# A later planned place for two kinds of stores, and a last product, join and store in two halves of rows

## The chip, the cores and the metric

One core of a Trainium2 chip runs the whole program. The metric is the time of one execution on the device, in microseconds (us); the runs of a kernel are given by their median. A profile of one more execution gives the trace. TensorE (PE) does the matmuls, VectorE (DVE) and ScalarE (ACT) the elementwise work, GpSimd (POOL) a little, and SyncE (SP) issues every DMA of this kernel from one queue, in order.

## The reference, cut to what matters

```python
x = chunk_attention(q, k, v)            # 8 x 8 heads, 576 tokens, chunks of 64, head size 64
x = concat_heads(x)                     # 8 x 576 x 512: 4608 tokens of 512
xn = layernorm(x) * g_ln
x = x + relu(xn @ w_ch1) @ w_ch2        # 512 -> 2048 -> 512
gate = sigmoid(causal_conv5(x, conv_w)) # five taps per channel, along the tokens
out = (gate * (x @ w_val)) @ w_out      # 512 -> 512 -> 512
```

All of it is float32. Every product is made from operands split into a high and a low part, with three matmuls (high by high, high by low, low by high).

## The kernel before, in words

**Blocks.** The 4608 tokens are nine blocks of 512. Blocks 0 and 1 go through the feed-forward layer with plain products. Blocks 2 to 8 use a scheme of seven products of half-size matrices in place of eight: `hidden` for the first matrix, and in the last stage `val` for `w_val` and `proj` for `w_out`. One such product is `twelve` (L1248): two column halves `f` of the left operand, two `k`, three high and low pairs, so 12 matmuls of 256 columns into one PSUM tile of 512 columns, 256 for each `f`. With the tokens' operand on the left, as in `proj`, `f` is the half of the rows (128 tokens each) of the result.

**What is stored and read again.** When a block leaves the feed-forward layer, `conv(b)` (L1613) works on its rows X in the background of the next blocks. For each of four groups of channels ScalarE starts the sum of taps in a room `u0` or `u1` (L1638), VectorE adds the other taps (L1645), and a store puts the result, the gate before its sigmoid, into DRAM (L1658). The next group but one takes the same room and must wait until that store has landed. `seven` (L1434) makes the block's seven operands for `val`: VectorE subtracts quadrants into `t` (L1454), ScalarE takes the high part (L1472), VectorE the low part (L1477), and a store puts the operand into DRAM (L1482); three rooms (`SPLITS`) take turns. Block 0 does the same later from a stored copy (`seven_again`, `conv_again`, stores at L1482 and L1600). When conv and operands of block b are done, X is free for block b + 2, whose attention tiles are copied there (L813 on ScalarE, L826 on GpSimd). `hidden` loads the half-size parts of the feed-forward weights again for each block (L1327, `late_a<-a`).

**What sets the order.** Nothing is ordered by hand. A planner (`Plan.run`, L55) simulates the engines: each operation has an engine, a duration, a priority (`pri`, a due time) and operations that it depends on. At each planned moment a free engine takes the ready operation of lowest priority value, and its instructions are emitted then; so the planned times set the order of every engine's queue, SP's among them, and the chip runs each queue in that order. Between an operation and one that waits for it on another engine the planner puts a fixed time:

```python
HOP = {"PE": 220.0, "DVE": 80.0, "ACT": 80.0, "POOL": 200.0, "SP": 3500.0}
wait = 0.0 if a.eng == (e,) else max(self.HOP[e], self.HOP["PE"] if "PE" in a.eng else 0.0) + op.more
if e == "SP":
    wait += a.slack
```

So a store is planned 80 ns behind VectorE's last operation on it. A store of the conv is planned at 728 ns and taken as landed 3500 ns behind that; one of an operand at 1300 ns and landed 3500 + 2000 ns behind that (its `more`).

**The end.** `proj(8)` does its seven products in the order 1, 5, 6, 3, 7, 4, 2. The last three results are: `c21` of product 4, copied by ScalarE and stored with `c22` as the lower 256 tokens (512 KB); `c12`, stored alone (256 KB); and `c11`: product 2 in the bank of `yB`, one VectorE operation that adds it to what ScalarE had copied (`join`, L1990), and one store of 256 tokens by 256 columns (256 KB, L1999).

Of the kernel before, what the change touches and what calls it, by code (L numbers as in the profile page):

```python
# [15 lines left out]
ALU = mybir.AluOpType  # L16
AX = mybir.AxisListType

P = 128
# [1 line left out]


class Op:
    __slots__ = ("eng", "dur", "fn", "deps", "pri", "left", "after", "ready", "seq", "xfer", "more", "slack")

    def __init__(self, eng, dur, fn, deps, pri, seq):
        self.eng, self.dur, self.fn, self.pri, self.seq = eng, dur, fn, pri, seq
        self.deps = [d for d in dict.fromkeys(deps) if d is not None]
        self.after, self.ready, self.xfer, self.more, self.slack = [], 0.0, None, 0.0, 0.0


class Plan:
# [10 lines left out]
    def add(self, eng, dur, fn, deps=(), pri=0.0, xfer=None):  # L43
        op = Op(eng if isinstance(eng, tuple) else (eng,), dur, fn, deps, pri, len(self.ops))
        op.xfer = xfer
        self.ops.append(op)
        return op
# [5 lines left out]
    def hold(self, tag, *ops):  # L53
        self.held[tag] = list(ops)

    def run(self):
        for op in self.ops:
            op.left = len(op.deps)
            for d in op.deps:
                d.after.append(op)  # L60
        free = {e: 740.0 if e == "SP" else 0.0 for op in self.ops for e in op.eng}
        ready = {e: [] for e in free}
        events = []
        done = set()

        def offer(op):
            for e in op.eng:
                heapq.heappush(ready[e], (op.pri, op.seq, op))

        for op in self.ops:  # L70
            if not op.left:
                offer(op)
        t, n, moved, landed = 0.0, 0, 0.0, []
        while n < len(self.ops):
            for e in free:
                if free[e] > t:
# [12 lines left out]
                dur = op.dur[op.eng.index(e)] if isinstance(op.dur, tuple) else op.dur  # L89
                end = t  # L90
                for x, parts in op.xfer or ():
                    flying = landed[-self.LANES :]
                    if len(flying) == self.LANES:
                        end = max(end, flying[0][0])
                    for l, _ in flying:
                        if sum(m for z, m in flying if z > end) + parts > self.RING:
                            end = max(end, l)
                    turn = self.TURN if parts == P and landed and landed[-1][1] != P else 0.0
                    end += dur
                    moved = max(end + self.LAG, moved + turn) + x  # L100
                    landed.append((moved, parts))
                if not op.xfer:
                    end = t + dur
                free[e] = end
                if len(op.eng) > 1:
                    op.fn(e)
                else:
                    op.fn()
                n += 1
                for a in op.after:  # L110
                    if op.xfer:
                        wait = moved - end
                    else:
                        wait = 0.0 if a.eng == (e,) else max(self.HOP[e], self.HOP["PE"] if "PE" in a.eng else 0.0) + op.more
                        if e == "SP":
                            wait += a.slack
                    a.ready = max(a.ready, end + wait)
                    a.left -= 1
                    if not a.left:
                        heapq.heappush(events, (a.ready, a.seq, a))  # L120
                heapq.heappush(events, (free[e], -1, None))
            if n == len(self.ops):
                break
            t = max(t, events[0][0])
            while events and events[0][0] <= t:
                op = heapq.heappop(events)[2]
                if op is not None:
                    offer(op)
# [3 lines left out]
def chunk_attention_ffn_gated_conv(  # L132
# [21 lines left out]
    nc = tc.nc  # L154
# [1090 lines left out]
        for kk in range(KD):  # L1245
            hold(f"W{g}_{kk}", *(last_use[g, x] for x in range(KD)), *reads)

    def twelve(ps, left, right, new):  # L1248


        for f in range(2):
            for k in range(2):
                lh, ll = (left(s, k)[:, f * P : (f + 1) * P] for s in range(2))
                for i, (l, r) in enumerate(((lh, 0), (lh, 1), (ll, 0))):
                    nc.tensor.matmul(  # L1255
                        ps[:, f],
                        l,
                        right(r, k),
                        start=new and f == k == i == 0,
                        stop=k == 1 and i == 2,  # L1260
                        skip_group_check=True,
                    )
# [169 lines left out]
    def seven(b, quad, reads, pri):  # L1432
# [29 lines left out]
        def split(i, m, src, *deps):  # L1462
            rt, sp = SPLITS[n_split[0] % 3], {}
            n_split[0] += 1

            def sources():
                return quad(*src) if src else [(0, HB, st["t"])]

            def high():
                sp["t"] = slot(rt, [P, 2, 2, HB], F32R, f"x7_{b}_{m}")  # L1470
                for lo, hi, a in sources():
                    nc.scalar.activation(out=sp["t"][:, 0, :, lo:hi], in_=a, func=AF.Copy)  # L1472

            def low():
                t = sp["t"]
                for lo, hi, a in sources():
                    nc.vector.tensor_tensor(  # L1477
                        out=t[:, 1, :, lo:hi], in0=a, in1=t[:, 0, :, lo:hi].bitcast(F32), op=ALU.subtract
                    )

            def store():
                nc.sync.dma_start(out=x7_dram[b, m].bitcast(F32), in_=sp["t"].bitcast(F32))  # L1482

            oh = add("ACT", 680, high, list(deps) + take(rt), pri)
            ol = add("DVE", 690, low, [oh], pri)
            x7_store[b, m] = add("SP", 1300, store, [ol], pri)
            x7_store[b, m].more = 2000.0
            hold(rt, x7_store[b, m])
            if src:
                last.setdefault(src, []).append(ol)  # L1490
            return ol
# [79 lines left out]
    def conv_again(f):  # L1571
# [35 lines left out]
            oa = add("DVE", 760, more(i), [oa], pri)  # L1607
        hold(rt, oa)
        conv_store[0, f] = add("SP", 728, keep, [oa], pri)
        hold(at, conv_store[0, f])  # L1610

    def conv(b):
# [19 lines left out]
        for f in range(KD if b else 0):  # L1632
# [31 lines left out]
                oa = add("DVE", 760, more(i), [oa], pri)  # L1664
            last.append(oa)
            conv_store[b, f] = add("SP", 728, keep, [oa], pri)
            hold(at, conv_store[b, f])
        if b == 0:
            x2_store[b] = add("SP", 2900, store, done, pri)
# [289 lines left out]
    def proj(jj):  # L1959
# [1 line left out]
        pri = B0 + SET * (jj + 1) + 5 * M_TIME  # L1961
        st, ends = {}, jj == NBLK - 1

        def product(m, into, new, deps):
            def go():
                if new:
                    st[into] = half_of(f"y{into.upper()}", f"o{j}_{m}")
                twelve(st[into], gv_o[j, m], wo[m], new)

            at = pri + 2 * M_TIME * (LAST_ORDER if ends else P_ORDER).index(m)  # L1970
            o = add("PE", 1385, go, [gv_op[j, m]] + wo_op[m] + deps, at)
            hold(gv_room[j, m], o)
            return o

        rooms = [OUT_RING[(out_n[0] + x) % len(OUT_RING)] for x in (0, 2 if ends else 1)]
# [11 lines left out]

            return add("ACT", 620, go, list(deps), pri - 1e7)

        def join(into, h, f, *deps):  # L1990
            def go():
                nc.vector.tensor_tensor(out=o(h, f), in0=o(h, f), in1=st[into], op=ALU.add)

            return add("DVE", 700, go, deps, pri - 1e7)

        def store(h, x, *deps):
            def go():
                r0 = j * NB + h * NB // 2
                nc.sync.dma_start(  # L1999
                    out=out[r0 : r0 + NB // 2, x].rearrange("(i p) d -> p i d", p=P), in_=st["o", h][:, :, x]  # L2000
                )

            hold(rooms[h], add("SP", 1300, go, deps, pri))
# [12 lines left out]
        store(1, slice(0, DM), c21, c22)  # L2016
        m3 = product("3", "b", False, [m5, s5])
        c12 = join("b", 0, 1, m3, u2)
        m2 = product("2", "b", True, [c12])
        c11 = join("b", 0, 0, m2, s1)  # L2020
        hold("yA", c21)
        hold("yB", c11)
        if ends:
            store(0, slice(DM // 2, DM), c12)
            store(0, slice(0, DM // 2), c11)
        else:
            store(0, slice(0, DM), c11, c12)


    g_op = ln_scale()  # L2030
# [80 lines left out]
```

## Time and profile before

| what | us |
|---|---|
| runs: median (lowest to highest of 3) | 1070.41 (1068.2 to 1075.63) |
| the profiled execution's own time | 1070.03 |
| its span in the trace | 1068.2 |
| PE busy in the span | 1053.9 |

The span runs from the first to the last instruction of the trace; 1.83 us of the profiled execution lie around it. A busy time is the time in which an engine had an instruction in work; matmuls overlap one another in it. In a row of waits the figures are the sum in us, the number of times and the longest one.

### The profile page before, as it was taken

Reading aid. Unit: us, or ns where it says so; the run is one execution under the profiler, and the core shown is the slowest. Engines: PE = TensorE matmul, PEld = TensorE weight load, DVE = VectorE, ACT = ScalarE, POOL = GpSimd, SP = SyncE. Lnnn points to the kernel's source line nnn. Section 1 sums busy time; section 2 is a strip of 40 time slices with the busy share of each in tenths; the row PEclk is TensorE's granted clock in tenths of the full one; section 3 lists DMA queues with packets and bytes.
Section 4 is the critical chain, followed back from the end, with each engine's and each line's share of the span. In section 5 each row is a group of like instructions: output and inputs, shape, how many; then the busy total and the mean of one; then the engine's idle time right before and its main releaser. Section 6 shows DMA issues by size and latency. Waiting matters only on the chain.

```text
span 1068.2 us, 22725 instructions
## 1 busy us (share of the span) xinstructions
PE 1053.9 (99%) x8950; PEld 951.4 (89%) x8950; DVE 856.4 (80%) x1464; ACT 540.3 (51%) x871; POOL 40.4 (4%) x77
## 2 busy tenths in 40 slices
PE   9999999999999999999999999999999999999998
PEld 8988888888899988889888898899898989999998
DVE  5888978888885888767878877878756889998785
ACT  5796634435354445445445543544443555655553
POOL 1011000000000000000000000000000000000000
PEclk9999999999999999999999999999999999999999
DMA  8995358667999899989989989998976988999852
GB/s 193 289 368 175 108 159 252 220 179 207 246 329 270 233 297 337 282 242 344 278 260 329 299 233 233 352 282 250 319 234 203 381 330 305 309 334 377 316 206 80
DMA packets 205905, 284.14 MB, mean 266 GB/s; under 512 B 99278, under 2 KB 151014, under 8 KB 205798
## 3 DMA queue, kind: packets, MB, share of 16 engines
q1 hardware_dynamic: 205798, 282.68, 84.6%
q8 instruction: 71, 1.16, 0.5%
q14 instruction: 36, 0.29, 0.1%
HBM read 207.64 MB, written 67.63 MB: 258 GB/s over the span
## 4 chain that ended last, share of the span: by engine, by line
PE 88%; DMA 4%; issue 2%; DVE 2%; ACT 2%; SPq 1%; POOL 0%; DVEq 0%; ACTq 0%; POOLq 0%
PE m L1255 24%; PE o L1255 8%; PE v L1255 8%; PE y L1034 7%; PE yA L1412 5%; PE yA L1414 5%; PE yB L1412 5%; PE yB L1414 4%; PE yA L1413 4%; PE yB L1413 4%; PE att L631 3%; PE att L604 3%; PE h L1010 3%; PE h L1012 2%; PE h L1011 2%
## 5 line engine op out<-in xcount | busy, mean ns | idle before, releaser
L1255 PEld LDWEIGHTS m<-late,late_a 128*128 128x128 f32 x2352 | 296.3, 188 | 22.5 <-DVE c_hl L1354 6.1
L1255 PE MATMUL m<-late,late_a 128*128 128x256 f32 x2352 | 303.3, 280 | 7.1 <-DMA late_a<-a 3.1
L1645 DVE SCALAR_TENSOR_TENSOR u_room<-X,cw_sb,u_room 128x516 f32<-128x516 f32 (+1 forms) x128 | 95.1, 747 | 10.4 <-ACT u_room L1638 7.9
L1034 PE MATMUL y<-hh,w 128*128 128x512 f32 x224 | 70.9, 398 | 0.0
L1354 DVE TENSOR_TENSOR c_hh<-c_hh,m 128x512 f32<-128x512 f32 x56 | 38.4, 685 | 36.6 <-PE m L1255 22.9
L1347 ACT ACTIVATE c_hh<-m 128x512 f32<-128x512 f32 x56 | 33.4, 596 | 54.9 <-PE m L1255 54.7
L1412 PE MATMUL yA<-late_h,w 128*128 128x512 f32 x148 | 59.4, 401 | 0.0
L1412 PE MATMUL yB<-late_h,w 128*128 128x512 f32 x148 | 59.0, 399 | 0.0
L1414 PE MATMUL yB<-late_h,w 128*128 128x512 f32 x148 | 58.1, 393 | 0.0
L1414 PE MATMUL yA<-late_h,w 128*128 128x512 f32 x148 | 58.0, 392 | 0.0
L1413 PE MATMUL yA<-late_h,w 128*128 128x512 f32 x148 | 58.0, 392 | 0.0
L1413 PE MATMUL yB<-late_h,w 128*128 128x512 f32 x148 | 57.8, 390 | 0.0
L1034 PEld LDWEIGHTS y<-hh,w 128*128 128x128 f32 x224 | 40.8, 188 | 8.4
L1287 ACT ACTIVATE late<-xs 128x512 fp32r<-128x512 f32 x49 | 30.4, 628 | 35.1 <-PE m L1255 20.6
L1010 PE MATMUL h<-xnt,w 128*128 128x512 f32 x112 | 45.4, 405 | 0.0
L770 POOL TENSOR_TENSOR rstd<-ve,neg_half 128x1 f32<-128x1 f32 x36 | 24.7, 687 | 541.8 <-DVE ve L750 541.4
L1012 PE MATMUL h<-xnt,w 128*128 128x512 f32 x112 | 44.2, 395 | 0.0
L1011 PE MATMUL h<-xnt,w 128*128 128x512 f32 x112 | 44.2, 394 | 0.0
L1034 PE MATMUL y<-hl,w 128*128 128x512 f32 x112 | 44.0, 393 | 0.0
L1382 ACT ACTIVATE late_h<-c_hh 128x512 fp32r<-128x512 f32 x38 | 23.9, 630 | 38.9 <-DVE c_hh L1354 38.2
L678 ACT ACTIVATE p<-p 128x512 f32<-128x512 f32 x33 | 20.8, 630 | 41.6 <-DVE p L670 23.6
L699 ACT ACTIVATE pT<-px 128x1024 uint16<-128x1024 uint16 x28 | 38.5, 1374 | 6.3 <-DMA px<-ps 6.1
(272 smaller groups left out, 2440.0 us busy)
## 6 DMA issues: line engine op xcount, KB each, us to landing
late_a<-a SPq DMA_DIRECT2D x196, 512.0 KB, 5.6
x7d<-late_x SPq DMA_DIRECT2D x42, 512.0 KB, 5.9
late_a<-x7d SPq DMA_DIRECT2D x39, 512.0 KB, 5.4
raw<-in_moe_w_ch_dram SPq DMA_DIRECT2D x32, 512.0 KB, 7.6
late<-x7d SPq DMA_DIRECT2D x24, 512.0 KB, 5.5
qk_room<-in_q_dram SPq DMA_DIRECT2D x100, 112.0 KB, 5.2
qk_room<-in_k_dram SPq DMA_DIRECT2D x100, 112.0 KB, 4.1
x7d<-x SPq DMA_DIRECT2D x21, 512.0 KB, 5.6
```

Of the source, the lines that this page charges most:

```text
L699: nc.scalar.activation(out=t.bitcast(U16).rearrange("p (x s) -> p s x", s=2), in_=st["turned"], func=AF.Copy)
L1010: nc.tensor.matmul(ps, wh, xh, start=(kk == 0), stop=False)
L1011: nc.tensor.matmul(ps, wh, xl, start=False, stop=False)
L1012: nc.tensor.matmul(ps, wl, xh, start=False, stop=(kk == KD - 1))
L1034: nc.tensor.matmul(ps, w[:, s], x, start=opens and n == 0, stop=closes and n == 2, skip_group_check=not b)
L1255: nc.tensor.matmul(ps[:, f], l, right(r, k), start=new and f == k == i == 0, stop=k == 1 and i == 2, skip_group_check=True,)
L1347: nc.scalar.activation(out=st[tag], in_=st[into], func=AF.Copy)
L1354: nc.vector.tensor_tensor(out=st[tag], in0=st[tag], in1=y, op=op)
L1412: nc.tensor.matmul(ps, wh, hh, start=opens and f == 0, stop=False)
L1413: nc.tensor.matmul(ps, wl, hh, start=False, stop=False)
L1414: nc.tensor.matmul(ps, wh, hl, start=False, stop=closes and f == 3)
L1645: nc.vector.scalar_tensor_tensor(out=a, in0=X[b][:, f, i : i + L], scalar=cw_sb[:, i, f : f + 1], in1=a, op0=ALU.mult, op1=ALU.add,)
```

## The change

Operations get a field `behind`, zero by default. Where an operation of another engine than SP ends, each operation that waits for it is planned later by its own `behind`. Three kinds of store get 2000 ns: the operands of `seven` (63 stores), the gates of `conv` and those of `conv_again` (36 stores, some in two DMAs). In the last block `proj` makes product 2 as two operations of six matmuls, one for each half of the rows; behind each half stand a VectorE join of 128 partitions by 256 elements and a store of 128 KB. The other blocks keep the product whole.

```diff
                         if e == "SP":
                             wait += a.slack
+                        else:
+                            wait += a.behind
...
             x7_store[b, m] = add("SP", 1300, store, [ol], pri)
+            x7_store[b, m].behind = 2000.0
             x7_store[b, m].more = 2000.0
...
         conv_store[0, f] = add("SP", 728, keep, [oa], pri)
+        conv_store[0, f].behind = 2000.0
...
             conv_store[b, f] = add("SP", 728, keep, [oa], pri)
+            conv_store[b, f].behind = 2000.0
...
-    def twelve(ps, left, right, new):
-        for f in range(2):
+    def twelve(ps, left, right, new, sides=(0, 1)):
+        for f in sides:
...
-            o = add("PE", 1385, go, [gv_op[j, m]] + wo_op[m] + deps, at)
-            hold(gv_room[j, m], o)
+            o = add("PE", 1385 * len(sides) // 2, go, [gv_op[j, m]] + wo_op[m] + deps, at)
+            if 1 in sides:
+                hold(gv_room[j, m], o)
...
-                nc.vector.tensor_tensor(out=o(h, f), in0=o(h, f), in1=st[into], op=ALU.add)
+                t = o(h, f)[:, side]
+                nc.vector.tensor_tensor(out=t, in0=t, in1=st[into][:, side], op=ALU.add)
...
         if ends:
             store(0, slice(DM // 2, DM), c12)
-            store(0, slice(0, DM // 2), c11)
+            m2 = product("2", "b", True, [c12], (0,))
+            c11 = join("b", 0, 0, m2, s1, side=slice(0, 1))
+            store(0, slice(0, DM // 2), c11, side=slice(0, 1))
+            m2 = product("2", "b", True, [m2], (1,))
+            c11 = join("b", 0, 0, m2, s1, side=slice(1, 2))
+            store(0, slice(0, DM // 2), c11, side=slice(1, 2))
         else:
+            m2 = product("2", "b", True, [c12])
+            c11 = join("b", 0, 0, m2, s1)
             store(0, slice(0, DM), c11, c12)
```

## Rows read from the trace of the kernel before

**Rows 1.** The page: its first line and the busy times by engine.
```profile
span 1068.2 us, 22725 instructions
...
PE 1053.9 (99%) x8950; PEld 951.4 (89%) x8950; DVE 856.4 (80%) x1464; ACT 540.3 (51%) x871; POOL 40.4 (4%) x77
```

**Rows 2.** Waits of PE, whole span: us in total, times, longest.
```profile
PE m L1255 <- DMA late_a<-a: 3.1, 2, 1.6
PE m L1255 <- DVE c_hl L1354: 2.1, 3, 1.0
...
PE m L1255 <- DVE c_hh L1354: 0.5, 1, 0.5
```

**Rows 3.** Waits of SP's queue, whole span.
```profile
SPq L1482 <- DVE late_x L1477: 12.3, 15, 1.8
...
SPq L1658 <- DVE u_room L1645: 9.7, 7, 2.4
...
SPq L1525 <- DMA gd<-u_room: 3.3, 1, 3.3
```

**Rows 4.** Line 1658, the conv's stores: issues and landing.
```profile
L1658 SPq DMA_DIRECT2D gd<-u_room x60: 319/422/1597, 268.7 to 948.3; - x60
...
DMA to landing us min/median/max: 2.5/4.7/7.6
```

**Rows 5.** Timeline, 670 to 679 us: start, us, engine, line, operation [idle before].
```profile
670.99 0.86 SPq L1658 DMA_DIRECT2D gd<-u_room  x2
...
671.95 0.44 SPq L1327 DMA_DIRECT2D late_a<-a  x1
...
678.15 3.06 PE L1255 MATMUL m<-late,late_a 128*128 128x256 f32 x24 [1.46 <-DMA late_a<-a]
```

**Rows 6.** Timeline of SP, 389 to 391 us.
```profile
389.31 0.38 SPq L1525 DMA_DIRECT2D u_room<-x2d  x1
389.78 0.89 SPq L1658 DMA_DIRECT2D gd<-u_room  x2
390.77 0.42 SPq L1327 DMA_DIRECT2D late_a<-a  x1
```

**Rows 7.** Waits, all engines, whole span: ScalarE for the conv's room.
```profile
ACT u_room L1638 <- DMA gd<-u_room: 25.8, 10, 5.8
```

**Rows 8.** Timeline, 549 to 562 us.
```profile
552.98 0.87 SPq L1658 DMA_DIRECT2D gd<-u_room  x2
...
558.48 0.73 ACT L1638 ACTIVATE u_room<-X,cw_sb 128x516 f32<-128x516 f32 x1 [2.39 <-DMA gd<-u_room]
...
561.45 0.74 PE L1255 MATMUL m<-late,late_a 128*128 128x256 f32 x4 [0.49 <-DVE c_hh L1354]
```

**Rows 9.** Timeline, 467 us: PE.
```profile
467.42 1.69 PE L1255 MATMUL m<-late,late_a 128*128 128x256 f32 x12 [0.96 <-DVE c_hl L1354]
```

**Rows 10.** Timeline of the end, 1062 to 1068.2 us.
```profile
1062.67 1.57 PE L1255 MATMUL o<-w,late_gv 128*128 128x256 f32 x12
...
1063.49 0.37 SPq L1999 DMA_DIRECT2D out_dram<-os  x1
1064.28 0.69 DVE L1992 TENSOR_TENSOR late_os<-late_os,o 128x512 f32<-128x512 f32 x1 [2.14 <-PE o L1255]
1065.00 0.37 SPq L1999 DMA_DIRECT2D out_dram<-late_os  x1
```

**Rows 11.** DMA issues, 1060 to 1068.2 us: number, KB each, us to landing.
```profile
out_dram<-late_os SPq DMA_DIRECT2D x2, 256.0 KB, 2.2
out_dram<-os SPq DMA_DIRECT2D x1, 512.0 KB, 2.8
```

**Rows 12.** Groups by line and shape: a VectorE operation of 256 elements out of PSUM.
```profile
L844 DVE TENSOR_TENSOR xnt<-att,xnt 128x256 fp32r<-128x256 f32 x8 | 3.0, 418 | 0.5 <-ACT X L813 0.3
```

**Rows 13.** Timeline, 675 to 690 us: last use of X, next block's last tile.
```profile
675.55 0.55 DVE L1454 TENSOR_TENSOR t<-X 128x384 f32<-128x384 f32 x1
...
689.99 0.60 PE L604 MATMUL att<-ident,x 128*128 128x128 f32 x4
```

More of the change, by code (lines that the diff above doesn't have):

```diff
@@ L23 @@
 class Op:
-    __slots__ = ("eng", "dur", "fn", "deps", "pri", "left", "after", "ready", "seq", "xfer", "more", "slack")
+    __slots__ = ("eng", "dur", "fn", "deps", "pri", "left", "after", "ready", "seq", "xfer", "more", "slack", "behind")
     def __init__(self, eng, dur, fn, deps, pri, seq):
@@ L28, in __init__ @@
         self.deps = [d for d in dict.fromkeys(deps) if d is not None]
-        self.after, self.ready, self.xfer, self.more, self.slack = [], 0.0, None, 0.0, 0.0
+        self.after, self.ready, self.xfer, self.more, self.slack, self.behind = [], 0.0, None, 0.0, 0.0, 0.0
 class Plan:
@@ L1962, in proj, with product @@
         st, ends = {}, jj == NBLK - 1
-        def product(m, into, new, deps):
+        def product(m, into, new, deps, sides=(0, 1)):
             def go():
-                if new:
+                if new and 0 in sides:
                     st[into] = half_of(f"y{into.upper()}", f"o{j}_{m}")
-                twelve(st[into], gv_o[j, m], wo[m], new)
+                twelve(st[into], gv_o[j, m], wo[m], new, sides)
             at = pri + 2 * M_TIME * (LAST_ORDER if ends else P_ORDER).index(m)
-            o = add("PE", 1385, go, [gv_op[j, m]] + wo_op[m] + deps, at)
-            hold(gv_room[j, m], o)
+            o = add("PE", 1385 * len(sides) // 2, go, [gv_op[j, m]] + wo_op[m] + deps, at)
+            if 1 in sides:
+                hold(gv_room[j, m], o)
             return o
@@ L1988, in shot, with join, store @@
             return add("ACT", 620, go, list(deps), pri - 1e7)
-        def join(into, h, f, *deps):
+        def join(into, h, f, *deps, side=slice(0, 2)):
             def go():
-                nc.vector.tensor_tensor(out=o(h, f), in0=o(h, f), in1=st[into], op=ALU.add)
-            return add("DVE", 700, go, deps, pri - 1e7)
-        def store(h, x, *deps):
+                t = o(h, f)[:, side]
+                nc.vector.tensor_tensor(out=t, in0=t, in1=st[into][:, side], op=ALU.add)
+            return add("DVE", 700 if side == slice(0, 2) else 400, go, deps, pri - 1e7)
+        def store(h, x, *deps, side=slice(0, 2)):
             def go():
@@ L1999, in go @@
                 nc.sync.dma_start(
-                    out=out[r0 : r0 + NB // 2, x].rearrange("(i p) d -> p i d", p=P), in_=st["o", h][:, :, x]
+                    out=out[r0 + side.start * P : r0 + side.stop * P, x].rearrange("(i p) d -> p i d", p=P),
+                    in_=st["o", h][:, side, x],
                 )
@@ L2018, in proj @@
         c12 = join("b", 0, 1, m3, u2)
-        m2 = product("2", "b", True, [c12])
-        c11 = join("b", 0, 0, m2, s1)
         hold("yA", c21)
-        hold("yB", c11)
         if ends:
             store(0, slice(DM // 2, DM), c12)
-            store(0, slice(0, DM // 2), c11)
-        else:
+            m2 = product("2", "b", True, [c12], (0,))
[4 more added lines that the diff above has]
+            store(0, slice(0, DM // 2), c11, side=slice(1, 2))
+        else:
+            m2 = product("2", "b", True, [c12])
+            c11 = join("b", 0, 0, m2, s1)
             store(0, slice(0, DM), c11, c12)
+        hold("yB", c11)
     g_op = ln_scale()
```

## The prediction

> **What bounds the kernel now.** I read the page's busy times first, then the waits of PE, then those of SP's queue, then short timelines around the places where PE waited, and the end last. The reader is to see in the busy times that PE is in work for 1053.9 of 1068.2 us [rows 1], so no more than 14.3 us of idle PE exists in the whole span, and the matmuls are the same before and after. The change touches neither their number nor their size. What it can win is a part of these 14.3 us.
>
> Where are they? At the end: the last matmul ends at 1062.67 + 1.57 = 1064.24 [rows 10], 3.96 us before the span's end. In the middle: PE's waits on loads of weights (3.1 us in 2) and on VectorE's joins (2.1 and 0.5 us in 4) [rows 2], 5.7 us together, all of them between 390 and 678 us. The first conv store is issued at 268.7 us [rows 4], and up to the first changed store the plan is the same, so the rest of the idle time (14.3 - 3.96 - 5.7 = 4.6 us, nearly all of it before that store) stays. The reach of the first part of the change is 5.7 us, that of the second a part of 3.96.
>
> **Part one, stores planned 2 us later: what it removes on SP.** SP issues in order, so a store that the plan puts 80 ns behind VectorE, and whose VectorE operation is late on the chip, holds up every load behind it. The waits of SP show that: 12.3 us in 15 and 9.7 us in 7 on the very operations that make the stored data [rows 3]. That is 22.0 us in 22 waits, a mean of 1.0 and a longest of 2.4. A store planned 2.0 us later covers all but some 0.4 us of the longest. So I expect most of these 22 us to go. SP's time is not the kernel's, though: what counts is which load was late for PE.
>
> There are two such loads. At 670.99 us the conv's store goes out, SP having waited the 2.4 us of its longest wait for VectorE's last tap [rows 3]; the weights behind it are issued at 671.95 and PE then stands 1.46 us until 678.15 [rows 5]. With the store out of the way the load goes out by the wait and the two store issues, 2.4 + 0.9 = 3.3 us, sooner, which is more than PE's 1.46: I take off 1.5. The other one is at 390.77: SP had waited 3.3 us [rows 3] at a load of the stored copy (389.31) whose room an earlier conv store had to leave, and then issued a store of its own (0.89 us) ahead of the weights [rows 6]. PE's share is 3.1 - 1.5 = 1.6. Here the change moves both the store and the load that hangs on it; whether the weights pass them is open, so I take half, 0.8.
>
> **What it removes on ScalarE and VectorE.** The room of a conv store is planned free 80 + 728 + 3500 ns = 4.3 us behind VectorE's last tap. On the chip the landing alone takes 4.7 us from the issue (median, up to 7.6) [rows 4], and the issue comes late. So ScalarE, in order, waits 25.8 us in 10 for the room [rows 7], and VectorE's joins, which PE needs, stand behind. One case: the store goes out at 552.98, ScalarE gets the room at 558.48 after 2.39 us of waiting, VectorE's join comes behind two taps, and PE stands 0.49 us at 561.45 [rows 8]. With 2.0 us more in the plan most of a mean wait of 2.6 us is gone. The joins' waits of PE are 2.1 + 0.5 = 2.6 us in 4; the longest (0.96) lies at 467 us [rows 9], where no conv operation stands ahead of the join, so 1.6 us hang on the rooms. I take three quarters, 1.2.
>
> **What part one adds.** No instruction, no byte. But every order behind the first changed store is planned anew, and a new order has its own gaps. The one gap among the six that hangs on neither a store nor a room is worth 1.0 us; I set 1.0 us for new ones (bounds: 0, and the 5.7 that the order of now has). The rooms are held longer in the plan: `u0` and `u1`, each used twice for a block, and `SPLITS`, three rooms for seven operands. That is four turns of 2.0 us, 8 us at most, by which X is released later. This is hidden as long as attention of the next block has slack: at 676 us X is released (675.55 + 0.55), the last tile of the block is turned at 689.99 [rows 13], 13.9 us later, with one tile's attention between. Were that cover gone, PE would stand at the block's start (rival three). Nothing is queued behind a store that has not yet been issued, so SP pays nothing.
>
> Part one: -1.5 - 0.8 - 1.2 + 1.0 = -2.5 us, bounds -5.7 and 0 for this mechanism alone.
>
> **Part two, the end in halves.** Now: PE ends 1064.24, the join runs 1064.28 to 1064.97 (0.69), the store is issued at 1065.00 and lands 2.2 us later [rows 10, 11], at 1067.2; a closing part of 1.0 us follows. PE's 12 matmuls stay 12; a join and a DMA issue are added. A join of 256 elements out of PSUM takes 0.42 [rows 12]. A store of 512 KB lands in 2.8 us, of 256 KB in 2.2 [rows 10], so I estimate 1.9 for 128 KB (lower bound), and 2.2 as the upper bound.
>
> Two cases. If the first half's join runs beside the second half's matmuls, only the second join is behind PE: 1064.28 + 0.42 + 0.03 = 1064.73 for the last issue, landing 1066.6 to 1066.9, so -0.3 to -0.6. If both joins come after the last matmul, the last issue is at 1064.28 + 0.42 + 0.03 + 0.42 + 0.03 = 1065.18, landing 1067.1 to 1067.4, so -0.1 to +0.2. Which? The plan emits the second six matmuls right at the end of the first (same engine, no hop), the first join 220 ns later, so PE is not held up. But both halves lie in one PSUM tile, and the last join starts 0.04 us behind the last matmul of the whole product [rows 10]; no row shows VectorE reading a tile that PE still writes. I take the second case, -0.1. Even in the first, the 512 KB store issued at 1063.49 lands only at 1066.3 [rows 10, 11] and moves its bytes on the same DMA engines, so little more would come.
>
> The Trainium skill speaks to this place: "PSUM — Partial Sum Buffer", section "PSUM bank collisions raise a hardware error", says that TensorE writing and VectorE reading one bank at the same time is an error even at different columns, and that accesses are to be guarded by bank. By that rule 512 fp32 columns, both halves, are one bank, the joins are kept behind all twelve matmuls, and the end gains 0.1; without it, up to 0.6. No run so far shows it either way.
>
> **The sum.** -2.5 - 0.1 = -2.6 us against the profiled execution: 1070.0 - 2.6 = 1067.4, span 1065.6. The median of the runs shown is 0.4 above the profiled execution and the lowest 1.8 below it, so a new median may lie that much off.
>
> **The rivals.**
>
> *Two: nothing that shows.* SP's waits shrink, but the new order has as many gaps as the old. For it: PE is 99% busy, and only 3.1 us of PE's waits are on loads although SP waited 22 us, so nearly all of SP's waits are already hidden. Against it: two PE gaps can be traced to a held queue or room, link by link. Time: 1070.0, with 1069 to 1071.
>
> *Three: slower, by the release of X.* Mechanism: conv and operands of each block end up to 8 us later, attention of the next block but one starts its last tile later, its operands are late, and PE stands at the block's start. It decides from the point where the delay passes the slack in the 13.9 us of [rows 13]; the one tile of attention in it would have to be squeezed. Price: six such releases, each with a stall of the size of the longest PE wait seen, 1.6 us, is 9.6; less the gain of 2.6 that stays, +7.0: 1077.0. For it: ScalarE already waits for rooms [rows 7]. Against it: on the chip the store already lands later than planned, so of the 8 us planned a good part only makes the plan true.
>
> *Four: the halves overlap and all five removable waits go, with no new gap.* -1.5 - 1.6 - 1.6 - 0.5 = -5.2: 1064.8.
>
> **How the numbers follow.** Forecast 0.52 (1066 to 1069); rival two 0.26; rival three 0.13 (1073 to 1082); rival four 0.09. The range 1064.0 to 1073.0 holds the forecast, two and four and the lower edge of three; about 0.15 is outside, nearly all above. Of 1%, about what a measurement of this kernel can tell from no change, 10.7 us, the idle time within reach (5.7 + 0.6) gives no way to be faster, so 0.01 for what I don't see; slower by over 1% is the upper part of rival three, 0.04; same 0.95.
>
> **What would show each step right or wrong.** SP's two waits of [rows 3] on L1477 and L1645 fall from 22 us to under 8; if not, the planned time does not carry to the chip. ScalarE's wait for the conv's room falls from 25.8 us to under 12. PE's waits between 268 and 980 us sum to about 3 rather than 5.7 us. At the end the first half's join starts only behind the last matmul, the last store is issued near 1.0 us behind it, and the time from last matmul to span's end is 3.7 to 4.1 us. PE waits of over 1 us at the start of several blocks would make it rival three; PE waits of 5 us or more in total with SP's waits gone would make it rival two.

## The result and the profile after

The changed kernel takes 1076.62 us (median of 13 runs, 1071.96 to 1083.51); the kernel before, beside it, 1070.41. The ratio is 1.0075 with a 95% interval of 1.006 to 1.009: slower by 0.75%, less than the 1% set as the bound, and on the other side of no change than forecast. The profiled execution took 1077.91 us, 7.9 more than the one before.

The page of the kernel after: its first line and the busy times, which answer to [rows 1].

```profile
span 1076.1 us, 22725 instructions
...
PE 1057.7 (98%) x8950; PEld 954.3 (89%) x8950; DVE 857.7 (80%) x1465; ACT 540.3 (50%) x871; POOL 40.1 (4%) x77
```

The count of instructions is that of before; VectorE has one more, the second join. Span minus PE busy is 18.4 us in place of 14.3: 4.1 of the 7.9 us are new idle time of PE, and 3.8 are the same 8950 matmuls taking longer. Nearly all of the second part is a lower granted clock (below). PE's waits after, between 250 and 1000 us, beside [rows 2] (us in total, times, longest):

```profile
PE m L1257 <- DMA late_a<-a: 5.0, 4, 1.9
PE m L1257 <- ACT c_hl L1349: 2.3, 2, 1.7
PE att L633 <- DMA v<-in_v_dram: 1.4, 1, 1.4
PE m L1257 <- DVE c_hl L1356: 1.0, 1, 1.0
PE m L1257 <- DVE c_hh L1356: 0.3, 1, 0.3
```

They sum to 10.0 us where 5.7 were before. Loads are the larger part in both (5.0 + 1.4 of 10.0 now, 3.1 of 5.7 before); waits on ScalarE's copies and on a load of v are new. Next SP's queue, beside [rows 3] (the stores of operands are L1484 now, those of gates L1662, the loads of block 0's stored copy L1528):

```profile
SPq L1528 <- DMA gd<-u_room: 9.4, 2, 6.0
SPq L1484 <- DMA late_a<-a: 9.3, 7, 2.0
...
SPq L1662 <- DVE u_room L1649: 2.7, 3, 1.0
...
SPq L1484 <- DVE late_x L1479: 1.9, 3, 0.9
```

The reader is to see a trade. What the change aimed at happened: the 22.0 us of SP's waits on VectorE fell to 2.7 + 1.9 = 4.6. (The prediction's count left out the same stores' waits under other names, 7.2 us for operands in `x` and 2.7 for block 0's gates; these are 0.3 us and none now.) But the wait of a load for a gate store's landing, 3.3 us before, is now 9.4 in two, and at the stores of operands SP has 9.3 us of waits put down to loads of weights, 3.9 before. ScalarE's wait for the room of the conv fell only from the 25.8 us of [rows 7] to 20.1, and its wait for the rooms of the operands rose from 2.4 us to 11.4, so that the two sum to 31.5 in place of 28.2. The operands' row before, and both rows after:

```profile
ACT late_x L1472 <- DMA x7d<-late_x: 2.4, 3, 1.1
```

```profile
ACT u_room L1642 <- DMA gd<-u_room: 20.1, 10, 4.0
ACT late_x L1474 <- DMA x7d<-late_x: 11.4, 8, 3.1
```

Where PE lost the time, by stretches (us; busy time and instructions of PE, PEld, DVE, ACT, POOL; PE's clock; share of the DMA engines; GB/s). First before, then after:

```profile
380.00:440.00 60.00, 58.39 (x493) 52.82 (x492) 47.16 (x81) 31.54 (x51) 2.60 (x4) 1.00 0.97 306
...
550.00:700.00 150.00, 146.90 (x1280) 131.48 (x1279) 119.62 (x204) 71.13 (x112) 6.28 (x10) 1.00 0.99 288
700.00:900.00 200.00, 200.00 (x1481) 180.30 (x1481) 155.64 (x269) 93.57 (x157) 3.67 (x6) 1.00 0.86 285
```

```profile
380.00:440.00 60.00, 56.78 (x457) 51.03 (x456) 46.03 (x78) 29.16 (x47) 2.60 (x4) 0.94 0.94 300
...
550.00:700.00 150.00, 145.43 (x1272) 130.23 (x1271) 118.00 (x204) 68.03 (x109) 6.49 (x11) 1.00 0.96 276
700.00:900.00 200.00, 198.90 (x1470) 178.86 (x1469) 154.10 (x265) 95.23 (x157) 3.67 (x6) 1.00 0.88 286
```

Idle PE rose by 1.6 us between 380 and 440, by 1.5 between 550 and 700 and by 1.1 between 700 and 900: 4.2, all of the new idle time. The clock is below full only in the first stretch, where 0.06 of 56.78 busy us is 3.4 of the 3.8 us.

That is one execution of each kernel. The clock falls in runs of both: its mean over the 13 runs of the changed kernel is 0.9978, and 0.9988 to 0.9991 over the four groups of runs of the kernel before that stand beside the experiments. A difference of 0.10 to 0.13% of the time that PE is busy is, by estimate, 1.1 to 1.4 us of the 6.2 us between the two medians. The 7.9 us of the profiled pair, with 3.4 of clock, overstate the clock's part.

The place that [rows 6] showed before, in the timeline of after:

```profile
384.54 1.77 SPq L1662 DMA_DIRECT2D gd<-u_room  x2
392.31 0.38 SPq L1528 DMA_DIRECT2D u_room<-x2d  x1
392.78 0.42 SPq L1329 DMA_DIRECT2D late_a<-a  x1
...
396.97 2.35 PE L1257 MATMUL m<-late,late_a 128*128 128x256 f32 x13 [1.86 <-DMA late_a<-a]
397.62 0.37 SPq L1528 DMA_DIRECT2D u_room<-x2d  x1
```

SP has issued the gate store at 386.3 and does nothing until 392.3: the next entry of its queue is a load into the same room, which must wait until the store has landed. That is the 6.0 us of its longest wait, and the weights stand behind it. The other 3.4 us stand ahead of the load at 397.62.

What this cost PE is smaller than SP's wait, and most of it is not at this place. The wait at 396.97 was there before, at 396.87, with 1.61 us: the weights now leave at 392.78 in place of 390.77, 2.0 us later, but land in 4.05 us in place of 5.96, and PE's wait grew by 0.25. The other 1.36 us are a new wait on the loads of v, which left at 413.53 before and leave 4.2 us later now:

```profile
417.74 2.60 SPq L593 DMA_DIRECT2D v<-in_v_dram  x4
...
423.26 0.96 PE L633 MATMUL att<-v,pT 64*64 64x64 f32 x10 [1.36 <-DMA v<-in_v_dram]
```

Between 550 and 700 us PE's long waits are three: 1.50 on weights at 589.79, 1.70 on a copy of ScalarE at 634.21, and 1.08 on weights at 684.78. The last is the wait of [rows 5]: the same product, ahead of the same tile of attention, where PE had stood 1.46 us at 678.15.

```profile
675.36 3.18 SPq L1329 DMA_DIRECT2D late_a<-a  x3
...
684.78 1.65 PE L1257 MATMUL m<-late,late_a 128*128 128x256 f32 x12 [1.08 <-DMA late_a<-a]
```

The load that it waits for, the second of the three, left at 675.99, 7.7 us before PE ran out of work; in [rows 5] it was 4.7 us. So it did leave 3.0 us sooner. But it landed in 8.66 us and not in 6.07, and the gain was 0.4. At 634.21 the copy stood behind another wait of ScalarE, on a DMA transpose of attention and not on the conv's room:

```profile
632.38 1.34 ACT L701 ACTIVATE pT<-px 128x1024 uint16<-128x1024 uint16 x1 [4.13 <-DMA px<-ps]
```

**Why the plan does that** can be read in the lines quoted ahead of the prediction. The 3500 ns of landing are added only where the waiting operation is on another engine; with `a.eng == (e,)` the wait is 0. A gate store and the load of the stored copy are both SP's, so for the planner the load is ready the moment the store has been issued, and it goes into the queue directly behind it. Planned 80 ns behind VectorE, the store drew the load to one place; planned 2 us later, it draws it to another. Of the terms in these lines only the load's own `slack` (zero here) could part them.

The end, beside [rows 10]:

```profile
1070.65 1.57 PE L1257 MATMUL o<-w,late_gv 128*128 128x256 f32 x12
...
1071.47 0.37 SPq L2006 DMA_DIRECT2D out_dram<-os  x1
1072.26 0.75 DVE L1999 TENSOR_TENSOR late_os<-late_os,o 128x256 f32<-128x256 f32 x2 [2.14 <-PE o L1257]
1072.71 0.85 SPq L2006 DMA_DIRECT2D out_dram<-late_os  x2
```

Both joins start behind the last of the twelve matmuls (1070.65 + 1.57 = 1072.22). From there to the span's end it is 3.9 us, 0.08 less than before.

### The profile page after: what moved, and what is told of

It reads as the page before. It is cut to its first block, busy times and chain, and to the rows that moved or that the text cites. A ratio compares the mean times of both kernels' runs of the same rounds, so it can differ in the third digit from the quotient of the medians.

```text
span 1076.1 us, 22725 instructions
## 1 busy us (share of the span) xinstructions
PE 1057.7 (98%) x8950; PEld 954.3 (89%) x8950; DVE 857.7 (80%) x1465; ACT 540.3 (50%) x871; POOL 40.1 (4%) x77
## 4 chain that ended last, share of the span: by engine, by line
PE 81%; DMA 11%; SPq 4%; DVE 2%; issue 1%; ACT 1%; DVEq 0%; POOL 0%; ACTq 0%
PE m L1257 21%; PE o L1257 8%; PE v L1257 8%; PE y L1036 7%; DMA late_a<-a 4%; PE yA L1414 4%; PE yA L1416 4%; PE yA L1415 4%; PE yB L1414 4%; PE yB L1416 4%; PE yB L1415 4%; PE att L633 3%; PE att L606 3%; PE h L1012 3%; PE h L1014 2%; PE h L1013 2%
```

## The experiments

Fourteen kernels; the table has them in the order in which they ran. A diff that takes a `behind` line away, changes its number or shows it without a sign is against the changed kernel, any other against the kernel before; the slack line goes into the kernel that is named with it. The results together (ratio to the kernel before, run beside it, with its 95% interval and the number of its runs; idle is span less PE busy of the profiled execution):

| kernel | ratio | runs | idle us | PE busy us |
|---|---|---|---|---|
| before | 1 | 13 | 14.3 | 1053.9 |
| after | 1.0075 (1.006 to 1.009) | 13 | 18.4 | 1057.7 |
| halves only | 1.0004 (0.9984 to 1.0024) | 10 | 13.6 | 1053.4 |
| operand stores only | 1.0008 (0.9992 to 1.0024) | 10 | 15.7 | 1054.5 |
| gate stores only | 1.0040 (1.0012 to 1.0068) | 10 | 22.0 | 1057.0 |
| after, loads with slack | 1.0013 (0.9995 to 1.003) | 10 | 15.4 | 1058.7 |
| before, rooms planned later | 1.0029 (1.0004 to 1.0055) | 10 | 21.4 | 1057.6 |
| before, loads with slack | 0.9966 (0.9943 to 0.999) | 10 | 11.7 | 1052.7 |
| operand stores, slack | 0.9990 (0.9965 to 1.0016) | 10 | 11.5 | 1056.3 |
| after with 3000 ns | 1.0089 (1.0056 to 1.0121) | 5 | 20.6 | 1055.6 |
| halves, slack | 0.9975 (0.996 to 0.9991) | 12 | 11.7 | 1052.9 |
| gate stores, slack | 1.0037 (1.0017 to 1.0057) | 8 | 15.4 | 1054.2 |
| after with 50 ns | 1.0007 (0.9994 to 1.0021) | 10 | 15.2 | 1053.2 |
| after with 1000 ns | 1.0090 (1.0071 to 1.0109) | 4 | 20.1 | 1056.9 |
| gate stores, slack, rooms as before | 1.0091 (1.0064 to 1.0117) | 5 | 21.5 | 1056.3 |
| before, slack, rooms planned later | 1.0037 (1.0011 to 1.0062) | 11 | 15.5 | 1058.4 |

The last two columns are one execution each, and it need not be a middle one: the 1080.80 us of "before, rooms planned later" are the longest of its ten runs, 8.3 above their median, and "gate stores only" and "after, loads with slack" lie 4.5 and 4.4 us above theirs.

### Which part of the change

**Halves only**: the change without its three `behind` lines.

```diff
-            x7_store[b, m].behind = 2000.0
-        conv_store[0, f].behind = 2000.0
-            conv_store[b, f].behind = 2000.0
```

> Only the last product, its join and its store in halves; no store is planned later. All theories agree that the loss is not here: the time from the last matmul to the span's end stays 3.9 us (3.96 before, 3.88 after the whole change), PE's waits are those of before, the time is 1070.3 within 0.2%.

**Operand stores only**, the last product whole:

```diff
             x7_store[b, m] = add("SP", 1300, store, [ol], pri)
+            x7_store[b, m].behind = 2000.0
```

> Only the 63 stores of the seven operands planned 2 us later, the product whole. Theory A (the loss comes from the conv's gate stores, behind which two loads of the stored copy wait on SP for a landing that the plan does not count): SP's wait of L1528 stays near 3.3 us, PE's waits in the middle stay at 4 to 6 us, the time is 1068 to 1071. Theory B (any new order of the plan has its own gaps, and that of before was a lucky one): PE's waits in the middle are 8 us or more and the time 1073 or more here too.

**Gate stores only**, the last product whole:

```diff
         conv_store[0, f] = add("SP", 728, keep, [oa], pri)
+        conv_store[0, f].behind = 2000.0
...
             conv_store[b, f] = add("SP", 728, keep, [oa], pri)
+            conv_store[b, f].behind = 2000.0
```

> Only the 36 gate stores planned 2 us later, the product whole. Theory A: SP's wait of L1528 rises to 6 us or more as after the whole change (9.4), PE waits 1.5 us or more behind it near 395 us, the granted clock falls below 1.00 just behind it, the time is 1074 to 1078. Theory B: somewhere between 1070 and 1080, with the gaps at other places.

1071.53, 1071.10 and 1076.31 us against 1071.26. The halves and the operand stores each cost nothing that can be told from zero; the gate stores alone are slower by 0.40%, with an interval above zero, and their idle time, 22.0 us, is longer than that of the whole change (18.4). So the gates carry the loss. The three ratios add up to 0.52% where the whole is 0.75%; the intervals are too wide to say whether the parts add.

Theory A has a miss in both kernels. With the operand stores alone SP's wait at the loads of the stored copy did not stay near 3.3 us: it is 7.1 in two, and PE is idle for 3.0 us between 380 and 440 us, as in the whole change (3.2). Yet the clock stays at 1.00 there, and no loss shows in the time. With the gate stores alone that wait is 5.4 us and not 6; PE's 2.5 us near 399, the clock of 0.97 and the time came as expected. So a longer wait of SP at these loads does not by itself make the kernel slower.

### The load behind the store

**After, with 6 us of slack for the loads of the stored copy**: the planner now puts them at least 6 us behind the store that they wait for.

```diff
             o = add("SP", 1300, go, [x2_store[0], *deps], pri)
             o.more = 1500.0
+            o.slack = 6000.0
             return o
```

> The whole change, and the loads of the stored copy in seven_again planned 6 us behind the store that they wait for, where the plan had put nothing between the two. Theory A: SP's wait of L1528 falls from 9.4 to under 3 us, the PE wait near 395 us (1.9) and the fall of the granted clock behind it go, the time falls by 4 to 6 us to 1071 to 1073. Theory B: the place near 395 us mends, other gaps open, the time stays 1074 to 1079.

1071.43 us. SP's wait at these loads is gone, and the stretch that had lost 1.6 us of idle time and 3.4 of clock has lost neither:

```profile
380.00:440.00 60.00, 60.00 (x499) 54.07 (x499) 49.11 (x86) 32.94 (x54) 3.15 (x5) 1.00 1.04 318
```

Between 550 and 700 us it is idle for 4.0 us, nearly as long as after (4.6), so this is not the only cause. With the slack 0.75% becomes 0.13%.

**Before, with the same slack** (the same one line). The load stood behind the store in the kernel before too, for 3.3 us.

> The kernel before, and the loads of the stored copy in seven_again planned 6 us behind the store that they wait for; no store is moved. Theory A: SP's wait of 3.3 us at L1525 goes, PE's wait of 1.6 us near 396 us goes, the time is 1067 to 1070. Theory B: 1072 or more.

1066.61 us, 0.34% faster than the kernel before and a little under the expected range. Set against this kernel and not against the one before, the change with slack is still slower by 0.5% (1.0013 to 0.9966): much of what the slack takes off the change it takes off the kernel before too. The loads now stand behind three loads of weights, as SP's timeline of this kernel shows:

```profile
386.78 0.90 SPq L1659 DMA_DIRECT2D gd<-u_room  x2
387.77 0.45 SPq L1327 DMA_DIRECT2D late_a<-a  x1
...
390.10 0.32 SPq L1327 DMA_DIRECT2D late_a<-a  x1
...
392.85 0.32 SPq L1327 DMA_DIRECT2D late_a<-a  x1
393.23 1.66 SPq L1525 DMA_DIRECT2D u_room<-x2d  x2
```

**Operand stores with slack, and the halves with slack**: the same line in the first two kernels.

> Only the operand stores planned 2 us later (1071.1 by themselves), and the loads of the stored copy planned 6 us behind their store; the product whole. Theory A: SP's waits at L1528 (7.1 us) and PE's idle time of 3.0 us between 380 and 440 us go, the time is 1067 to 1070, under the kernel before. Theory B: 1071 or more, with other gaps.

> No store planned later; the loads of the stored copy planned 6 us behind their store (0.9966 by itself), and the last product in halves. All theories: the halves add or take 0.1 us at most, the time is 1065 to 1068, and this is the fastest version.

1069.53 and 1066.35 us; PE is never idle between 380 and 440 us in either. The halves with slack are, with the slack alone, the best kernels seen; nothing separates these two.

### The rooms

**Before, with the rooms planned free 2 us later and the stores left where they were.** `more` is added to the landing for operations of other engines alone, so this delays ScalarE's next start in the room and nothing else.

```diff
         conv_store[0, f] = add("SP", 728, keep, [oa], pri)
+        conv_store[0, f].more = 2000.0
...
             conv_store[b, f] = add("SP", 728, keep, [oa], pri)
+            conv_store[b, f].more = 2000.0
```

> The kernel before, and the landing of the gate stores (not the stores themselves) planned 2 us later: 5.5 us behind the store for ScalarE, in place of 3.5. Theory A says that the changed kernel left ScalarE's wait for the conv's room at 20.1 us of 25.8 because a store planned later takes its planned landing along with it; then here the wait falls to under 12 us, and the time is 1068 to 1072. Theory B (every new order costs): 1073 or more, whatever the wait does.

1072.49 us. ScalarE's waits in this kernel:

```profile
ACT u_room L1639 <- DMA gd<-u_room: 5.2, 2, 4.2
```

The wait that the prediction wanted away is away, and the kernel is slower by 0.29%; the time lies between the ranges of the two theories. In the profiled execution, a long one, PE's idle time is 21.4 us, 6.4 of it between 550 and 700 us. There a load of weights that left at 582.2 landed 9.9 us later, and PE waited 3.9 us for it, the longest of its waits on `late_a`. SP's wait at a load of the stored copy rose too, from 3.3 to 5.8 us, and this kernel has no slack for it.

**Gate stores only, with slack**: the gates' two `behind` lines and the slack line.

> Only the gate stores planned 2 us later (1076.3 by themselves), with the loads of the stored copy planned 6 us behind their store; the product whole. Theory A with a second part (gate stores that go out later meet the operand stores and the weights on the DMA engines near 585 and 680 us): PE's idle time between 380 and 440 us goes, that between 550 and 700 us stays at 3 to 5 us with a weight load landing 8 us or more behind its issue, the time is 1070 to 1073. Theory A without it: 1066 to 1068, as the load alone. Theory B: anywhere from 1066 to 1076.

1073.24 us against 1069.43, a ratio of 1.0037. Against the 0.9966 of the slack alone, moving the gate stores costs 0.7% even where no load of the stored copy stands behind them. Against the gate stores without slack (1.0040) the slack brings nothing that these intervals can show, though PE's idle time between 380 and 440 us fell from 4.6 to 0.8. The time and the 2.8 us between 550 and 700 lie just outside what the second part of theory A gave; a load of weights landed there 8.05 us behind its issue, as it had it.

What is left can hang on the store's own later place or on the rooms, which it frees later. The last two kernels take these apart.

**Gate stores later, rooms planned as before, slack:**

```diff
         conv_store[0, f].behind = 2000.0
+        conv_store[0, f].more = -2000.0
...
             conv_store[b, f].behind = 2000.0
+            conv_store[b, f].more = -2000.0
```

> Gate stores planned 2 us later, but the rooms u0 and u1 planned free at the time of before (landing term shortened by 2 us), loads with 6 us of slack, last product whole. Theory A (the rest of the loss hangs on the rooms' later turn): about 1067, ratio below 0.999, PE idle between 550 and 700 us below 2 us. Theory B (it hangs on the later place of the store itself): about as with the later rooms, ratio 1.002 to 1.006, PE idle there 2.8 us or more. On the chip the store leaves later and the room with it, so ScalarE's wait for the room should grow above 25.8 us in either.

**Stores as before, rooms planned later, slack**: the two `more = 2000.0` lines and the slack line in the kernel before.

> Gate stores where before has them, the rooms planned free 2 us later, loads with 6 us of slack, last product whole. Theory A (the rooms): ratio 1.002 to 1.006, PE idle between 550 and 700 us 2.8 us or more. Theory B (the store's place): about 1067, ratio below 0.999, ScalarE's room wait near 5 us as with the longer landing alone.

1080.29 and 1074.56 us against 1069.45. With the slack, the four corners are 0.9966 (neither), 1.0037 (rooms), 1.0037 (both) and 1.0091 (stores, rooms as before). For the second kernel the rooms' theory holds (4.6 us idle between 550 and 700). For the first both theories missed: it was to fall below 0.999 or to lie at 1.002 to 1.006, and it is worse than either, with 2.5 us idle between 550 and 700 and 5.7 between 700 and 900. Its waits of PE show where:

```profile
PE m L1257 <- ACT c_hl L1349: 6.9, 4, 2.5
PE m L1257 <- DVE c_hl L1356: 3.4, 3, 1.7
PE m L1257 <- DVE h L1387: 1.3, 1, 1.3
```

and so do ScalarE's, where the expectation had more than 25.8:

```profile
ACT u_room L1643 <- DMA gd<-u_room: 46.5, 14, 5.4
```

One such wait, in its timeline:

```profile
553.63 0.86 SPq L1663 DMA_DIRECT2D gd<-u_room  x2
...
559.93 0.72 ACT L1643 ACTIVATE u_room<-X,cw_sb 128x516 f32<-128x516 f32 x1 [3.46 <-DMA gd<-u_room]
560.56 0.58 ACT L1349 ACTIVATE c_hl<-m 128x512 f32<-128x512 f32 x1
...
561.19 1.66 PE L1257 MATMUL m<-late,late_a 128*128 128x256 f32 x12 [2.45 <-ACT c_hl L1349]
```

The store goes out at 553.63, ScalarE stands 3.46 us for the room, the copy that PE needs is queued behind it and ends at 561.14, and PE has stood for 2.45 us. This is the chain of [rows 8], made longer: the store is later in fact, and the plan does not know it. Where only the plan has the room later, the chain is gone, and something else is late. In the second kernel ScalarE waits only this long,

```profile
ACT u_room L1640 <- DMA gd<-u_room: 3.6, 2, 2.9
```

and PE waits for weights in place of it. Its timeline:

```profile
577.24 1.74 SPq L1327 DMA_DIRECT2D late_a<-a  x2
579.08 3.39 SPq L563 DMA_DIRECT2D qk_room<-in_q_dram  x4
583.07 1.14 SPq L1660 DMA_DIRECT2D gd<-u_room  x2
...
587.83 2.87 PE L1255 MATMUL m<-late,late_a 128*128 128x256 f32 x12 [3.47 <-DMA late_a<-a]
```

The load issued at 577.8 landed 9.9 us later (the page's median for after is 5.9). In the kernel with the slack alone a load of weights at this place left at 575.0 and landed in 7.5; PE stood 0.9 us between 580 and 590. The load is not late in the queue: PE reaches this place 2.6 us later here as well, and both loads left 6.6 to 6.7 us before PE ran out of work. What differs is the landing. Over these landings the DMA engines were busy all the time in both kernels (shares 1.01 and 1.01), and moved 320 GB/s here and 393 in the kernel with the slack alone. Four q loads of 112 KB, two gate stores and a store of operands were issued while this load was under way; there it was two gate stores, two loads of weights and three stores of operands, and no q load. That the q loads held it up is argued from this and not tested.

### The size of the delay

**After with 3000, 50 and 1000 ns** in its three `behind` lines:

```diff
-            x7_store[b, m].behind = 2000.0
+            x7_store[b, m].behind = 3000.0
```

> The whole change with 3000 ns in place of 2000. Theory A: loads of the stored copy still stand directly behind a gate store in SP's queue, so SP waits 5 us or more at L1528 and the time is 1074 to 1079, as with 2000. Theory B: the time is anywhere between 1068 and 1082, the gaps at other places.

> The whole change with 50 ns in place of 2000: a small disturbance of the plan that moves no store by a time that the chip could tell. Theory A: as the kernel before, 1069 to 1072, ratio 0.998 to 1.002. Theory B (any disturbance of the plan costs as much as the change): 1074 or more.

> The whole change with 1000 ns in place of 2000. Theory A: the loads of the stored copy still stand behind a gate store; SP waits 4 us or more at L1528 and the time lies between before and after, 1071 to 1076. Theory B: no order by the size of the delay; it may lie under the kernel before or above the changed one.

1079.32, 1070.32 and 1078.74 us. A delay of 50 ns plans everything anew too and costs nothing that shows: the idea that any new order costs as much falls. From 1000 ns on the loss is there in full, 0.90%, 0.75% and 0.89% with overlapping intervals, and it does not grow with the delay: with 1000 ns the time was to lie between before and after, and does not, and with 3000 it is 0.3 us above its range. SP's waits at the loads of the stored copy are 8.7, 9.4 and 9.5 us at 1000, 2000 and 3000 ns and 3.6 at 50. That fits loads that are either caught at a bad place or not, and not a price per microsecond.

## Why the prediction was wrong

**What bounds the kernel** was read rightly, as a limit on gains: 14.3 us of idle PE, of which 5.7 in reach. It was no limit on losses. Idle time can be added, and the clock can fall, neither of which is bounded by the idle time of now.

**In the prediction's own terms** the idle time of the profiled pair adds up as follows, without the end.

| term | forecast us | measured us |
|---|---|---|
| wait on weights at 678, now at 684.78 | -1.5 | -0.4 |
| wait on weights at 396.9 | -0.8 | +0.25 |
| waits on VectorE's joins | -1.2 | -1.4 |
| new gaps | +1.0 | +5.7 |
| sum | -2.5 | +4.2 |

To this come 3.8 us by which PE was longer in work, most of it the clock, for which the prediction had no term.

**New gaps, +1.0, is the step that failed by most.** The prediction set it by "The one gap among the six that hangs on neither a store nor a room", that is, from an order made without the change. Five new waits sum to 5.7 us, the upper of the bounds it gave: 1.36 on v at 423, 1.50 on weights at 590, 1.70 and 0.59 on ScalarE's copies at 634 and 704, 0.52 on weights at 863. PE's waits came to 10.0 us where "about 3" was the sign.

**The half of the wait at 390.77, -0.8, failed too.** The prediction put it: "Here the change moves both the store and the load that hangs on it; whether the weights pass them is open, so I take half". They don't pass. The load came out directly behind the later store again, and SP stood for 9.4 us in place of 3.3. The bounds given for it had no loss in them: this wait of PE grew by 0.25 us, and the new one on v and 3.4 us of clock stand in the same stretch. With it falls the sentence "Nothing is queued behind a store that has not yet been issued, so SP pays nothing": a load that waits for that store's landing is queued behind it, and the quoted condition of the planner (no landing between two operations of one engine) says so. The slack, which parts the two, takes the whole loss from this stretch and brings the whole change from 1.0075 to 1.0013. It also brings the kernel before to 0.9966, so only some 0.3 of the 0.75% is the difference that these loads make between the two kernels, and some 0.5% stays when both have the slack; the intervals, 0.2 wide on either side, make this a rough division.

**The gap at 678 us, -1.5,** failed at the landing. SP's waits fell as the first sign asked (22.0 to 4.6, under 8 forecast), and the weights left 3.0 us sooner, near the 3.3 forecast. The prediction took it that they would then land as much sooner; they landed in 8.66 us in place of 6.07, and PE still waits 1.08 of its 1.46 us.

**The joins behind the rooms, -1.2,** came out near in size, but not by the way given: "With 2.0 us more in the plan most of a mean wait of 2.6 us is gone". The plan has no 2.0 us more for the landing: store and landing move together, and ScalarE's wait went from 25.8 to 20.1, not under 12. The size is luck as far as is known. Where the wait was taken away in earnest, it was not worth what was set on it: with `more` it fell to 5.2 and 3.6 us, and both kernels are slower than the same ones without it, by 0.29% (an interval from 0.04 to 0.55) and from 0.9966 to 1.0037.

**The end** came as worked out: both joins behind the last matmul, at 1072.26 against 1072.22; the last store issued at 1073.15, 0.9 us behind it (the second of the two in the row at 1072.71); two joins in 0.75 us where 0.84 was taken, a landing of 1.9 for 128 KB (the lower bound), 3.9 us to the span's end, a gain of 0.08 where 0.1 was forecast. The kernel with the halves only shows the same (joins at 1063.11, last matmul's end at 1063.06). The joins stayed behind all twelve matmuls as the rule in the Trainium skill would have it ("PSUM — Partial Sum Buffer", section "PSUM bank collisions raise a hardware error"). In the trace it is a wait for PE's signal (2.14 <-PE o), so the program keeps them apart; what a read beside the matmuls would do on the chip, no run here shows.

**The rivals.** Rival three had the right side and, by luck, nearly the time (1077.0). Its mechanism was not what was seen: its sign was PE waits at the start of several blocks, and the new idle time stands in waits on weights and on ScalarE's copies inside blocks. Its premise, that rooms planned free later cost time, is borne out by the two kernels with `more = 2000.0`, but there PE waits mostly for weights (5.4 and 5.1 us) and not for X. Rival two's second sign (5 us or more of PE waits with SP's waits gone) came true, with a time that it did not have. The range, up to 1073.0, ended 3.6 us short, because the moved stores were costed from what they would no longer delay, and not from what they, and the loads that hang on them, would now delay themselves.

Left open: why weights land so late near 590 and 684 us, where the new order issues other transfers beside them, and how the 0.75% divides between the loads of the stored copy and the rooms. The slack takes 0.6% off the change, 0.34% off the kernel before, and nothing that shows off the gate stores alone; that these three don't agree is within their intervals or is a third cause, and no run here tells which.

## What to carry to other kernels

When a store is moved in an in-order queue, look for the loads that wait for its landing and see where they stand in the same queue; parted from it by 6 us in the plan they made the kernel before 0.3% faster here. A load that leaves sooner need not land as much sooner (3.0 us gave 0.4 here). The ScalarE wait that was planned away (25.8 to 5.2 us) came back as a wait of PE on weights, so a stall on an engine off the bound is priced by what the bound engine waits for, and its removal by what runs in its place. And bound every moved operation from both sides: its landing and all that hangs on it move along.

## What the runs showed that was not expected

In these two executions the granted clock of PE fell after one gap and not after another of nearly the same length. In after, by 4 us stretches, around the 1.86 us gap at 395 and the one of 1.36 at 422 us:

```profile
394.00:398.00 4.00, 2.14 (x18) 1.98 (x17) 1.86 (x3) 0.86 (x2) 0.00 (x0) 0.98 0.60 221
398.00:402.00 4.00, 4.00 (x52) 3.87 (x53) 0.69 (x1) 1.53 (x3) 0.00 (x0) 0.59 0.74 229
422.00:426.00 4.00, 2.73 (x69) 2.56 (x70) 3.40 (x6) 2.64 (x6) 0.00 (x0) 0.90 1.06 380
426.00:430.00 4.00, 4.00 (x18) 3.54 (x18) 2.51 (x5) 2.15 (x4) 0.00 (x0) 0.68 1.00 338
```

and in before, behind its gap of 1.61 us at the same place:

```profile
394.00:398.00 4.00, 2.39 (x21) 2.23 (x21) 2.00 (x3) 1.01 (x2) 0.00 (x0) 1.00 0.96 387
398.00:402.00 4.00, 4.00 (x86) 3.62 (x85) 2.15 (x4) 2.23 (x4) 0.00 (x0) 1.00 1.03 416
```

A clock of 0.59 is a mean of full speed (2.4 GHz) and the half of it (1.2 GHz). The rows of after lose 0.41 x 4.00 + 0.32 x 4.00 + 0.10 x 2.73 = 3.2 us of full-speed work, and the two gaps themselves are 1.86 + 1.36 = 3.2 us: here a gap cost about as much by the clock as by itself. Behind the 3.47 us gap of the kernel with later rooms and slack the row from 588 to 592 us stands at 0.59 again. In the kernel with the operand stores alone, gaps of 1.53 and 1.31 us at the same two places left the stretch from 380 to 440 at 1.00. A sum of idle time is therefore too small a measure of a new gap, and the prediction had no term for it.
